# One sine table and its exchanged copy, in a two-dimensional Fourier mix with an RWKV channel mix

## The chip, the cores and the metric

The kernel runs on one core of one Trainium2 chip. The core has five engines that run their own instruction queues in order and meet through semaphores: TensorE (PE: matrix products from SBUF into PSUM, weight loads shown apart as PEld), VectorE (DVE), ScalarE (ACT, with tables for functions such as the sine and the sigmoid), GpSimd (POOL) and SyncE (SP, which only issues transfers here). DMA engines move data between HBM and SBUF; in this kernel the inputs are fetched from GpSimd's queue, except for two small vectors, and the outputs are written from SyncE's. The metric is the device time of one execution in microseconds; lower is better.

## The reference

```python
def _attn_ref(x):                      # x: 8 x 3072 x 256
    X = np.fft.fft(x, axis=1)
    X = np.fft.fft(X, axis=2)
    return X.real.astype(np.float32)

def _moe_ref(x, mu_k, mu_r, w_k, w_v, w_r):
    x_prev = np.concatenate([np.zeros((B, 1, D)), x[:, :-1, :]], axis=1)
    xk = mu_k * x + (1.0 - mu_k) * x_prev
    xr = mu_r * x + (1.0 - mu_r) * x_prev
    k = np.maximum(xk @ w_k, 0.0)      # 256 -> 1024
    v = k * k @ w_v                    # 1024 -> 256
    r = 1.0 / (1.0 + np.exp(-(xr @ w_r)))
    return (r * v).astype(np.float32)
```

The second function takes the output of the first.

## The kernel before

The sequence of 3072 is split into 48 x 64. For each of the 8 batches the Fourier transform is made of products with small tables of sines: `a_sum` (batch 0 and half of batch 1) or `butterfly` and `a_item` (the others) transform over 48 with the table `w_pm`; `d_half` and `d_item` transform over the 256 columns with `w_eo`; `c_item` transforms over the remaining 64 with the tables `m1` and `m2`, which have 27 slots of 64 columns on 128 partitions. Every one of these ends in an eviction from PSUM into SBUF (`evac`, lines 358 to 362) on ScalarE ("A") or VectorE ("V"). `d_item` n fills four of the 24 units of `g_all`, whose columns 0, 257 and 258 to 385 must be zero; `g_zeros` writes these zeros.

`halves` and `diff` then form the transform's rows and their differences, and `scaled` and `mixed` form the mixed inputs x of the channel mix, all on VectorE. The channel mix works on 48 chunks of 512 tokens (three per half `m` of a batch). A chunk takes four steps: each step has a `k_piece` (product with w_k, line 494; relu on ScalarE, line 498), each second step a `square` on VectorE (line 504); the first step of the next chunk has its `r_item` (product with w_r, line 511, sigmoid on ScalarE); and five steps behind, `v_tile` makes the product with w_v (line 523) and `v_out` multiplies by the sigmoid on VectorE and stores.

The order of all instructions is written out by hand. Lines 541 to 578 are the first work of batch 0, up to step 0. From there a table (`at(step, f, ...)`, lines 605 to 671) says which other items go into which step: in a step, `k_piece` comes first, then items on TensorE ("x"), then `v_tile`, then items on VectorE ("w"), then `v_out` and `square`. `pin_order` keeps every engine to this order.

PSUM has three large slots, taken in turn by `ps_w()`, and two small ones, taken in turn by `ps_v()`. A product waits until the eviction of the slot's former content is done. `keep_busy` puts products of zeros into the queue of TensorE between the first items.

The setup comes ahead of line 541. GpSimd issues the loads of batch 0 (line 106), fills `kcol_i` with integers (line 161) and computes angles as integers: for two tables and in two stretches of slots, 0 to 9 (`NS1`) and 9 to 27 (`m_angles`, line 274). VectorE wraps them to one turn (`m_wrap`, line 279) and ScalarE takes the sine (`m_sine`, line 283) into m1 and m2. The two tables differ by the phase that is added: on the lower 64 partitions a quarter and a half turn, on the upper 64 none and a quarter (before half a turn that all have). `m_rest` sets the slots that are exceptions. VectorE also computes `row_i` (lines 235 to 249), the row numbers by which GpSimd gathers w_k, w_r and part of mu (`gather`, line 321): the first half of the weights' rows (`m` = 0) first, then `load_xh(1, 0)`, w_r, w_v, `load_xh(1, 1)` and the other half (lines 324 to 341). `load_xh(b, h)` loads half h of batch b's x in two transfers. The other part of mu goes by six transfers from SyncE.

Of the kernel before, what the change touches and what calls it, by code (L numbers as in the profile page):

```python
# [9 lines left out]
FP32 = mybir.dt.float32  # L10
# [25 lines left out]
def kernel(  # L36
# [101 lines left out]
    def keep_busy(n):  # L138

        ps = ps_w()  # L140
        for _ in range(n):
            nc.tensor.matmul(out=ps[:, 0:512], lhsT=zeros[:, 0:P], rhs=zeros, start=True, stop=True)  # L142
# [37 lines left out]
    for c in range(2):  # L180
        phase(0.25 + 0.25 * c, 0.25 * c)
# [30 lines left out]
    for g in range(2):  # L212
        for n in range(2):
# [15 lines left out]
    V.tensor_scalar(out=rr_f, in0=rr_f, scalar1=float(TURN) / S, scalar2=None, op0=ALU.mult)  # L229

    row_f = const.tile([P, 4], FP32)
    row_i = const.tile([P, 4], UINT32)
    first = const.tile([P, 1], FP32)
    late = const.tile([P, 1], FP32)
    V.tensor_scalar(out=first, in0=pcol_f, scalar1=0.0, scalar2=None, op0=ALU.is_equal)
    V.tensor_scalar(out=late, in0=pcol_f, scalar1=65.0, scalar2=-127.0, op0=ALU.is_ge,
                    op1=ALU.mult)
    V.scalar_tensor_tensor(out=late, in0=pcol_f, scalar=2.0, in1=late, op0=ALU.mult,
                           op1=ALU.add)
    V.tensor_scalar(out=late, in0=late, scalar1=-1.0, scalar2=first, op0=ALU.add, op1=ALU.add)  # L240
    V.tensor_copy(out=row_f[:, 0:1], in_=late)
    V.tensor_scalar(out=late, in0=late, scalar1=-1.0, scalar2=256.0, op0=ALU.mult, op1=ALU.add)
    V.scalar_tensor_tensor(out=row_f[:, 1:2], in0=first, scalar=-128.0, in1=late,
                           op0=ALU.mult, op1=ALU.add)
    V.scalar_tensor_tensor(out=row_f[:, 2:3], in0=first, scalar=-256.0, in1=late,
                           op0=ALU.mult, op1=ALU.add)
    V.scalar_tensor_tensor(out=row_f[:, 3:4], in0=first, scalar=128.0, in1=row_f[:, 0:1],
                           op0=ALU.mult, op1=ALU.add)
    V.tensor_copy(out=row_i, in_=row_f)

    V.memset(mu_f, 0.0)
# [11 lines left out]
    ang = []  # L263
    for nm in ("rl", "k2"):
        t = k2_pool.tile([P, 8, 512], FP16, name=nm, tag=nm)
        ang.append(t.rearrange("p a b -> p (a b)").bitcast(INT32)[:, 0:NSL * 64]
                   .rearrange("p (s t) -> p s t", t=64))
    m1 = const.tile([P, NSL, 64], FP16)
    m2 = const.tile([P, NSL, 64], FP16)
    m_s = const.tile([P, 64], FP16)  # L270
# [450 lines left out]
```

## Time and profile before

| | us |
|---|---|
| median of 14 runs | 470.9 |
| lowest and highest run | 469.98 and 472.45 |
| the profiled execution's own time | 470.13 |
| its span | 468.3 |
| TensorE busy | 453.9 |
| VectorE busy | 358.7 |
| ScalarE busy | 358.3 |
| GpSimd busy | 38.4 |
| start of the first `k_piece` (line 494) | 22.96 |

The profile is of one execution. Times are counted from the start of its span. In the lists in order of time, a line has the start, the length, the engine, the line of the kernel, the operation, what it writes and reads, its count (neighbours are merged), and in brackets how long the engine was idle before it and what ended that. "issue" is idle time that no wait explains. A wait for several things is put down to the one that came last. In the lists by stretch, each engine has its busy time and, in brackets, its number of instructions; the last columns are TensorE's granted clock, the DMA engines' busy share and GB/s. DMA issue on GpSimd counts as its instruction; the transfer itself runs later.

### The profile page before, as it was taken

The numbers are of one execution on the slowest core, as the hardware profiler recorded it, in microseconds if no ns is written. First come the engines' busy times: TensorE is split into PE (matmuls) and PEld (weight loads), VectorE is DVE, ScalarE is ACT, GpSimd is POOL, SyncE is SP. The second block draws the span as 40 slices with busy tenths as digits, with TensorE's granted clock in tenths as the row PEclk, the third lists the DMA queues.
The fourth block names the chain that finished last, engine by engine and source line by source line (L and its number), as shares of the span: only waits on it lengthen the run. The fifth ranks groups of instructions, "written<-read, shape, count | busy, mean of one in ns | idle before, by whom it ended". The sixth has DMA issues, their size and how long they took to land.

```text
span 468.3 us, 10069 instructions
## 1 busy us (share of the span) xinstructions
PE 453.9 (97%) x4258; PEld 333.7 (71%) x4258; DVE 358.7 (77%) x496; ACT 358.3 (77%) x390; POOL 38.4 (8%) x60
## 2 busy tenths in 40 slices
PE   8759999999999999999999999999999999999996
PEld 5537777777777777777777777777777777776774
DVE  7878987987689867887679777897678854898443
ACT  4758898888777887788878887878877888666661
POOL 8850000000000010000000000000000000000000
PEclk9899999999999999999999999999999999999999
DMA  7692752535622365233732356233232222323333
GB/s 134 111 176 43 166 114 68 97 88 116 133 51 64 69 120 129 48 68 67 155 91 51 67 113 137 48 68 69 46 69 46 67 57 57 69 53 82 71 69 90
DMA packets 32561, 40.24 MB, mean 86 GB/s; under 512 B 4164, under 2 KB 30276, under 8 KB 31172
## 3 DMA queue, kind: packets, MB, share of 16 engines
q1 hardware_dynamic: 27812, 25.05, 22.9%
q0 software_dynamic: 4560, 14.42, 18.1%
q8 instruction: 33, 0.54, 0.5%
q10 hardware_dynamic: 144, 0.13, 0.1%
q14 instruction: 12, 0.10, 0.1%
HBM read 28.84 MB, written 25.17 MB: 115 GB/s over the span
## 4 chain that ended last, share of the span: by engine, by line
PE 95%; ACT 3%; DVE 1%; issue 0%; ACTq 0%
PE psV L523 36%; PE psW L494 35%; PE psW L511 9%; PE psW L398 4%; PE psW L425 4%; PE psW L374 4%; PE psW L388 1%; ACT a L362 1%; PE psW L142 1%; ACT pq L362 0%; ACT m L283 0%; ACT L597 0%; DVE y L437 0%; DVE a L360 0%; PE psV L398 0%
## 5 line engine op out<-in xcount | busy, mean ns | idle before, releaser
L498 ACT ACTIVATE rl<-psW 128x1024 f16<-128x1024 f32 x192 | 196.5, 1023 | 87.9 <-PE psW L494 87.9
L494 PE MATMUL psW<-x,wk 128*128 128x512 f16 x768 | 197.2, 379 | 1.8 <-ACT a L362 1.0
L523 PE MATMUL psV<-wv_sb,k 128*128 128x256 f16 x1536 | 198.6, 273 | 0.0
L504 DVE TENSOR_TENSOR k<-rl 128x2048 f16<-128x2048 f16 x96 | 117.4, 1223 | 65.2 <-ACT rl L498 64.6
L523 PEld LDWEIGHTS <-k 128*128 128x128 f16 x1536 | 143.9, 98 | 20.0
L494 PEld LDWEIGHTS <-wk 128*128 128x128 f16 x768 | 74.9, 98 | 52.3 <-issue 2.8
L531 DVE SCALAR_TENSOR_TENSOR o<-psV,r 128x512 f32<-128x512 f32 x96 | 66.1, 689 | 29.1 <-PE psV L523 28.0
L470 DVE TENSOR_TENSOR x<-y,t 128x1536 f16<-128x1536 f16 (+1 forms) x72 | 62.6, 870 | 2.5
L362 ACT ACTIVATE a<-psW 128x768 f16<-128x768 f32 x61 | 49.0, 807 | 6.4 <-PE psW L388 3.9
L511 PE MATMUL psW<-wr,x 128*128 128x256 f16 x384 | 49.8, 273 | 0.0
L516 ACT ACTIVATE r<-psW 128x1024 f16<-128x1024 f32 x48 | 48.9, 1019 | 0.8 <-PE psW L511 0.8
L511 PEld LDWEIGHTS <-x 128*128 128x128 f16 x384 | 37.5, 98 | 14.4 <-DVE x L470 0.2
L362 ACT ACTIVATE g_all<-psW 128x1024 f16<-128x1024 f32 (+1 forms) x46 | 46.7, 1019 | 0.3 <-PE psW L398 0.3
L106 POOL DMA_DIRECT2D xh<-in_x_dram x36 | 18.6, 522 | 242.8 <-DVE eo L119 229.5
L398 PEld LDWEIGHTS <-a 128*128 128x128 f16 x384 | 26.0, 100 | 11.8 <-issue 1.0
L119 DVE TENSOR_TENSOR eo<-xh 96x2048 f16<-96x2048 f16 x26 | 31.5, 1213 | 0.6 <-DMA xh<-in_x_dram 0.6
L374 PEld LDWEIGHTS <-eo 96*128 96x128 f16 x416 | 23.4, 97 | 11.6
L425 PEld LDWEIGHTS <-g_all 128*128 128x128 f16 x648 | 23.9, 99 | 9.3 <-issue 1.7
L362 ACT ACTIVATE pq<-psW 128x896 f16<-128x896 f32 (+5 forms) x33 | 28.6, 867 | 2.3 <-PE psW L398 1.7
L398 PE MATMUL psW<-w_eo,a 128*128 128x128 f16 x376 | 29.0, 222 | 0.7 <-issue 0.7
L425 PE MATMUL psW<-m,g_all 128*128 128x64 f16 x648 | 25.2, 195 | 2.2 <-ACT rl L498 1.4
L374 PE MATMUL psW<-w_pm,eo 96*128 96x96 f16 x416 | 26.3, 205 | 0.0
(87 smaller groups left out, 157.4 us busy)
## 6 DMA issues: line engine op xcount, KB each, us to landing
out_dram<-o SPq DMA_DIRECT2D x191, 128.0 KB, 2.4
xh<-in_x_dram POOLq DMA_DIRECT2D x28, 384.0 KB, 6.1
xh<-in_x_dram POOLq DMA_DIRECT2D x8, 192.0 KB, 5.9
wv_sb<-in_moe_w_v_dram POOLq DMA_DIRECT2D x1, 512.0 KB
out_dram<-o ACTq DMA_DIRECT2D x1, 128.0 KB, 2.8
wk<-in_moe_w_k_dram,row_i POOLq DMA_INDIRECT x4, 10.9
wr<-in_moe_w_r_dram,row_i POOLq DMA_INDIRECT x4, 9.1
mu_f<-in_moe_mu_k_dram SPq DMA_DIRECT2D x1, 0.0 KB
```

Source lines behind the costliest of these rows:

```text
L362: nc.scalar.activation(out=out_ap, in_=in_ap, func=AF.Copy)
L374: nc.tensor.matmul(out=ps[:, 128 * i:128 * i + 96], lhsT=eo[:, 8 * j + i, e, :], rhs=w_pm[0:96, 0], start=True, stop=True)
L398: nc.tensor.matmul(out=_v(ps, 256 * i + 64 * (1 - e), [(128, 2), (1, 64)]), lhsT=a_t[b][:, e, 2 * u:2 * u + 2, :], rhs=w_eo[:, e, :], star ...
L425: nc.tensor.matmul(out=ps[:, o + 64 * i:o + 64 * i + 64], lhsT=g_all[:, u, col:col + 128], rhs=m[:, sl], start=first, stop=last)
L470: V.tensor_tensor(out=dst, in0=_v(y_t[b], 64 * (NSL * a + lo + 3 * m), [(1, n)]), in1=_v(x_t["t", a], 64 * lo, [(1, n)]), op=ALU.subtract ...
L494: nc.tensor.matmul(out=ps[:, 512 * hs:512 * hs + 512], lhsT=wk_sb[m][a][:, 128 * fc:128 * fc + 128], rhs=xk[:, a, 512 * i:512 * i + 512], ...
L498: nc.scalar.activation(out=st["rl"][:, 2 * ds:2 * ds + 2], in_=ps.rearrange("p (f t) -> p f t", f=2), func=AF.Relu, bias=0.0, scale=0.25)
L504: V.tensor_tensor(out=k2_t[c][:, 2 * ds - 2:2 * ds + 2], in0=r, in1=r, op=ALU.mult)
L511: nc.tensor.matmul(out=ps[:, 256 * tb:256 * tb + 256], lhsT=x_t[b, 1, m][:, a, 512 * i + 128 * tb: 512 * i + 128 * tb + 128], rhs=wr_sb[m] ...
L516: nc.scalar.activation(out=st["r", c], in_=ps, func=AF.Sigmoid)
L523: nc.tensor.matmul(out=st["v"][:, 256 * h:256 * h + 256], lhsT=k2_t[c][:, fc, 128 * tb:128 * tb + 128], rhs=wv_sb[:, fc], start=(fc == 0), ...
L531: V.scalar_tensor_tensor(out=o.rearrange("p a b -> p (a b)"), in0=st["v"], scalar=16.0, in1=st["r", c][:, 256 * (tb - 1):256 * (tb + 1)], ...
```

## The change

The second table is no longer computed: `m_swap` makes it from the first, m2's lower 64 partitions being the negative of m1's upper, m2's upper 64 a copy of m1's lower. The angles, wraps and sines are made for one table. `row_i` is written column by column in `rows()`, which comes after the first wrap and sine of the first work; the loads come behind it in `loads()`. The angles of w_eo are made with one operation less, and ahead of the first wrap. The zeros of units 8 to 24 of `g_all` are written by GpSimd, between `load_xh(1, 0)` and the gather of w_r, not by VectorE. The sigmoid's table is loaded before step 0, not in step 1. `keep_busy` takes a small PSUM slot, and one call (of two products) goes. In the steps, `d_item` 4 is evicted by ScalarE, `a_sum(1, 0, 0)` is evicted by VectorE and comes in step 2, and `m_rest(1)` comes in step 0.

```diff
@@ -137,7 +137,7 @@
 
     def keep_busy(n):
 
-        ps = ps_w()
+        ps = ps_v()
         for _ in range(n):
             nc.tensor.matmul(out=ps[:, 0:512], lhsT=zeros[:, 0:P], rhs=zeros, start=True, stop=True)
 
@@ -177,8 +177,7 @@
             phs[lo, hi] = t
         return phs[lo, hi]
 
-    for c in range(2):
-        phase(0.25 + 0.25 * c, 0.25 * c)
+    phase(0.25, 0.0)
 
     pcol_f = const.tile([P, 1], FP32)
     hi48 = const.tile([P, 1], FP32)
@@ -227,28 +226,29 @@
                     op0=ALU.bitwise_and, op1=ALU.logical_shift_left)
     V.tensor_tensor(out=rr_f, in0=pos_h, in1=pos_l, op=ALU.add)
     V.tensor_scalar(out=rr_f, in0=rr_f, scalar1=float(TURN) / S, scalar2=None, op0=ALU.mult)
-
...
-    V.tensor_copy(out=row_i, in_=row_f)
-
-    V.memset(mu_f, 0.0)
+
+    def rows():
+        first = const.tile([P, 1], FP32)
+        late = const.tile([P, 1], FP32)
+        low = const.tile([P, 1], FP32)
+        high = const.tile([P, 1], FP32)
+        V.tensor_scalar(out=late, in0=pcol_f, scalar1=65.0, scalar2=-127.0, op0=ALU.is_ge,
+                        op1=ALU.mult)
+        V.tensor_scalar(out=first, in0=pcol_f, scalar1=0.0, scalar2=None, op0=ALU.is_equal)
+        V.scalar_tensor_tensor(out=late, in0=pcol_f, scalar=2.0, in1=late, op0=ALU.mult,
+                               op1=ALU.add)
+        V.tensor_scalar(out=low, in0=late, scalar1=-1.0, scalar2=first, op0=ALU.add,
+                        op1=ALU.add)
+        V.tensor_scalar(out=high, in0=low, scalar1=-1.0, scalar2=256.0, op0=ALU.mult,
+                        op1=ALU.add)
+        V.tensor_copy(out=row_i[:, 0:1], in_=low)
+        for n, v, by in ((1, high, -128.0), (2, high, -256.0), (3, low, 128.0)):
+            V.scalar_tensor_tensor(out=row_i[:, n:n + 1], in0=first, scalar=by, in1=v,
+                                   op0=ALU.mult, op1=ALU.add)
 
 
     NU = 24
@@ -260,85 +260,90 @@
         V.memset(g_all[:, u0:u1, 0:1], 0.0)
 
 
-    ang = []
-    for nm in ("rl", "k2"):
-        t = k2_pool.tile([P, 8, 512], FP16, name=nm, tag=nm)
-        ang.append(t.rearrange("p a b -> p (a b)").bitcast(INT32)[:, 0:NSL * 64]
-                   .rearrange("p (s t) -> p s t", t=64))
+    ang = (k2_pool.tile([P, 8, 512], FP16, name="rl", tag="rl")
+           .rearrange("p a b -> p (a b)").bitcast(INT32)[:, 0:NSL * 64]
+           .rearrange("p (s t) -> p s t", t=64))
     m1 = const.tile([P, NSL, 64], FP16)
     m2 = const.tile([P, NSL, 64], FP16)
-    m_s = const.tile([P, 64], FP16)
 
     def m_angles(s0, s1):
-        for c in range(2):
-            nc.gpsimd.tensor_scalar(out=ang[c][:, s0:s1], in0=kcol_i[:, s0:s1], scalar1=rr_f,
-                                    scalar2=phase(0.25 + 0.25 * c, 0.25 * c),
-                                    op0=ALU.mult, op1=ALU.add)
-
-    def m_wrap(c, s0, s1):
-        V.tensor_scalar(out=ang[c][:, s0:s1], in0=ang[c][:, s0:s1], scalar1=TURN - 1,
+        nc.gpsimd.tensor_scalar(out=ang[:, s0:s1], in0=kcol_i[:, s0:s1], scalar1=rr_f,
+                                scalar2=phase(0.25, 0.0), op0=ALU.mult, op1=ALU.add)
+
+    def m_wrap(s0, s1):
+        V.tensor_scalar(out=ang[:, s0:s1], in0=ang[:, s0:s1], scalar1=TURN - 1,
                         scalar2=None, op0=ALU.bitwise_and)
 
-    def m_sine(c, s0, s1):
-        nc.scalar.activation(out=(m2 if c else m1)[:, s0:s1], in_=ang[c][:, s0:s1],
-                             func=AF.Sin, bias=m_pi, scale=TWO_PI / TURN)
+    def m_sine(s0, s1):
+        nc.scalar.activation(out=m1[:, s0:s1], in_=ang[:, s0:s1], func=AF.Sin, bias=m_pi,
+                             scale=TWO_PI / TURN)
+
+    lo64, hi64 = slice(0, 64), slice(64, 128)
+
+    def m_swap(s0, s1):
+
+        V.tensor_scalar(out=m2[lo64, s0:s1], in0=m1[hi64, s0:s1], scalar1=-1.0, scalar2=None,
+                        op0=ALU.mult)
+        V.tensor_copy(out=m2[hi64, s0:s1], in_=m1[lo64, s0:s1])
 
     def m_rest(part):
 
 
 
-        h = slice(64, 128)
-        if part == 1:
-            V.tensor_copy(out=m_s[h], in_=m1[h, 25])
-            V.tensor_copy(out=m1[h, 25], in_=m2[h, 25])
-            V.tensor_scalar(out=m2[h, 25], in0=m_s[h], scalar1=-1.0, scalar2=None, op0=ALU.mult)
+        s = 26 if part else 0
+        if part:
+            V.tensor_scalar(out=m2[hi64, 25], in0=m1[hi64, 25], scalar1=-1.0, scalar2=None,
+                            op0=ALU.mult)
+            V.tensor_copy(out=m1[hi64, 25], in_=m1[lo64, 25])
         for m in (m1, m2):
-            s = 26 if part else 0
-            V.tensor_scalar(out=m[h, s], in0=m[h, s], scalar1=-1.0, scalar2=None, op0=ALU.mult)
+            V.tensor_scalar(out=m[hi64, s], in0=m[hi64, s], scalar1=-1.0, scalar2=None,
+                            op0=ALU.mult)
             if part:
-                V.memset(m[0:64, 25], 0.0)
+                V.memset(m[lo64, 25], 0.0)
             else:
-                V.memset(m[h, 1], 0.0)
+                V.memset(m[hi64, 1], 0.0)
                 V.memset(m[:, 0, 0:1], 0.0)
 
+
+    ueo = const.tile([P, 2, 2, 64], INT32)
+    w_eo = const.tile([P, 2, 128], FP16)
+    for c in range(2):
+        V.tensor_scalar(out=ueo[:, :, c], in0=veo_i[:, :, c], scalar1=pd_f,
+                        scalar2=(0.5 + 0.25 * c) * TURN, op0=ALU.mult, op1=ALU.add)
+    V.tensor_scalar(out=ueo, in0=ueo, scalar1=TURN - 1, scalar2=None, op0=ALU.bitwise_and)
     m_angles(0, NS1)
     kcol(NS1, NSL)
-    m_wrap(0, 0, NS1)
-    m_wrap(1, 0, NS1)
-
-    ueo = const.tile([P, 2, 2, 64], INT32)
-    w_eo = const.tile([P, 2, 128], FP16)
-    V.tensor_scalar(out=ueo, in0=veo_i, scalar1=pcol_f, scalar2=float(TURN) / D,
-                    op0=ALU.mult, op1=ALU.mult)
-    for c in range(2):
-        V.tensor_scalar(out=ueo[:, :, c], in0=ueo[:, :, c], scalar1=(0.5 + 0.25 * c) * TURN,
-                        scalar2=None, op0=ALU.add)
-    V.tensor_scalar(out=ueo, in0=ueo, scalar1=TURN - 1, scalar2=None, op0=ALU.bitwise_and)
-    g_zeros(0, 8)
+    m_angles(NS1, NSL)
 
 
     def gather(dst, w, n):
         nc.gpsimd.indirect_dma_start(dst, None, w,
                                      bass.IndirectOffsetOnAxis(ap=row_i[:, n:n + 1], axis=0))
 
-    m_angles(NS1, NSL)
-    for a in range(2):
-        gather(wk_sb[0][a], moe_w_k, a)
-    mus = [mu.rearrange("(a b) -> a b", b=1) for mu in (moe_mu_k, moe_mu_r)]
-    for i, mu in enumerate(mus):
-        nc.sync.dma_start(out=mu_f[0:1, 0, i:i + 1], in_=mu[0:1])
-        nc.sync.dma_start(out=mu_f[1:65, 0, i:i + 1], in_=mu[1:129:2][0:64])
-        nc.sync.dma_start(out=mu_f[65:128, 0, i:i + 1], in_=mu[2:128:2])
-        gather(mu_f[:, 1, i:i + 1], mu, 1)
-    load_xh(1, 0)
-    for a in range(2):
-        gather(wr_sb[0][a], moe_w_r, a)
-    nc.gpsimd.dma_start(out=wv_sb, in_=moe_w_v.rearrange("(fc p) v -> p fc v", p=128))
-    load_xh(1, 1)
-    for a in range(2):
-        gather(wk_sb[1][a], moe_w_k, 2 + a)
-    for a in range(2):
-        gather(wr_sb[1][a], moe_w_r, 2 + a)
+    def loads():
+
+        V.memset(mu_f, 0.0)
+        mus = [mu.rearrange("(a b) -> a b", b=1) for mu in (moe_mu_k, moe_mu_r)]
+        for i, mu in enumerate(mus):
+            nc.sync.dma_start(out=mu_f[0:1, 0, i:i + 1], in_=mu[0:1])
+            nc.sync.dma_start(out=mu_f[1:65, 0, i:i + 1], in_=mu[1:129:2][0:64])
+            nc.sync.dma_start(out=mu_f[65:128, 0, i:i + 1], in_=mu[2:128:2])
+        for a in range(2):
+            gather(wk_sb[0][a], moe_w_k, a)
+        for i, mu in enumerate(mus):
+            gather(mu_f[:, 1, i:i + 1], mu, 1)
+        load_xh(1, 0)
+        nc.gpsimd.memset(g_all[:, 8:24, 258:GU], 0.0)
+        for c in (0, 257):
+            nc.gpsimd.memset(g_all[:, 8:24, c:c + 1], 0.0)
+        for a in range(2):
+            gather(wr_sb[0][a], moe_w_r, a)
+        nc.gpsimd.dma_start(out=wv_sb, in_=moe_w_v.rearrange("(fc p) v -> p fc v", p=128))
+        load_xh(1, 1)
+        for a in range(2):
+            gather(wk_sb[1][a], moe_w_k, 2 + a)
+        for a in range(2):
+            gather(wr_sb[1][a], moe_w_r, 2 + a)
 
     def eo_sine():
         nc.scalar.activation(out=w_eo.rearrange("p a b -> p (a b)"),
@@ -541,32 +546,34 @@
 
     a_sum(0, 0, 0)
     a_sum(0, 0, 4)
+    m_wrap(0, NS1)
+    m_sine(0, NS1)
+    rows()
+    loads()
     keep_busy(3)
     a_sum(0, 0, 8)
     a_sum(0, 0, 12)
-    m_sine(0, 0, NS1)
-    m_sine(1, 0, NS1)
+    eo_sine()
+    m_swap(0, NS1)
+    g_zeros(0, 8)
+    m_wrap(NS1, NSL)
     keep_busy(2)
     a_sum(0, 1, 0)
-    m_wrap(0, NS1, NSL)
+    m_sine(NS1, NSL)
+    eo_rest()
     a_sum(0, 1, 4, "V")
-    eo_sine()
-    m_sine(0, NS1, NSL)
     keep_busy(2)
     a_sum(0, 1, 8, "V")
-    eo_rest()
     m_rest(0)
     a_sum(0, 1, 12)
-    keep_busy(2)
     d_half(0, 0, ps_v(), "A")
     d_half(0, 2, ps_v(), "V")
     d_half(0, 4, ps_w(), "A")
     d_half(0, 6, ps_w(), "V")
-    m_wrap(1, NS1, NSL)
+    m_swap(NS1, NSL)
     c_item(0, 0, 5)
     halves(0, 0, 5)
     c_item(0, 5, 4)
-    m_sine(1, NS1, NSL)
     halves(0, 5, 9)
     diff(0, 0, 8)
     d_item(0, 2)
@@ -574,7 +581,7 @@
         scaled(0, 0, 0, a, 0, 8)
         mixed(0, 0, 0, a, 0, 8)
     d_item(0, 3)
-    g_zeros(8, 24)
+    nc.scalar.activation(out=pd_f, in_=m_pi, func=AF.Sigmoid)
     keep_busy(6)
 
 
@@ -590,11 +597,6 @@
         for a in range(2):
             V.tensor_copy(out=mu_m[:, a], in_=mu_f[:, 1 - a])
         V.tensor_copy(out=mu_m[0:1], in_=mu_f[0:1])
-
-    warm = const.tile([P, 1], FP32)
-
-    def sigmoid_table():
-        nc.scalar.activation(out=warm, in_=m_pi, func=AF.Sigmoid)
 
     chunks = [(b, m, i) for b in range(B) for m in range(2) for i in range(3)]
     nk = 4 * len(chunks)
@@ -605,14 +607,13 @@
 
     at(0, c_item, 0, 9, 8)
     at(0, mix2, 0, 1, 0, 0, 8)
+    at(0, m_rest, 1)
     at(0, halves, 0, 9, 17)
     at(0, diff, 0, 8, 16)
-    at(1, sigmoid_table)
-    at(1, d_item, 0, 4, "V")
-    at(1, a_sum, 1, 0, 0)
+    at(1, d_item, 0, 4)
     at(1, mix2, 0, 0, 0, 8, 16)
     at(2, d_item, 0, 5)
-    at(2, m_rest, 1)
+    at(2, a_sum, 1, 0, 0, "V")
     at(3, c_item, 0, 17, 8)
     at(3, butterfly, 1, 1, 0)
     at(4, halves, 0, 17, 25)
```

## The prediction

> **What bounds the kernel now.** I read the first page, then the engines stretch by stretch, then the order of time of each engine up to 60 us, then the DMA packets by the microsecond.
>
> The page: the span is 468.3 us and TensorE is busy in nearly all of it.
>
> ```profile
> span 468.3 us, 10069 instructions
> PE 453.9 (97%) x4258; PEld 333.7 (71%) x4258; DVE 358.7 (77%) x496; ACT 358.3 (77%) x390; POOL 38.4 (8%) x60
> ```
>
> Busy time by stretch (length, then TensorE, weight loads, VectorE, ScalarE, GpSimd, granted clock, DMA share):
>
> ```profile
> 30.00:36.00 6.00, 2.50 (x31) 1.44 (x30) 5.14 (x14) 4.36 (x6) 0.53 (x1) 1.00 0.99 182
> 36.00:42.00 6.00, 6.00 (x58) 4.39 (x55) 4.63 (x9) 5.04 (x6) 0.00 (x0) 1.00 0.03 5
> 48.00:60.00 12.00, 12.00 (x115) 8.99 (x113) 11.83 (x18) 10.07 (x12) 0.00 (x0) 1.00 0.64 143
> ```
>
> From 36 us on TensorE has no idle time until the last microseconds. The change touches only what comes earlier, so its worth is how much earlier TensorE passes the places where something else can still hold it. The 48 to 60 row names that something: VectorE is busy 11.83 of 12.00 us there. In order of time:
>
> ```profile
> 35.19 1.22 DVE L119 TENSOR_TENSOR eo<-xh 96x2048 f16<-96x2048 f16 x1 [0.58 <-DMA xh<-in_x_dram]
> 36.71 1.23 DVE L504 TENSOR_TENSOR k<-rl 128x2048 f16<-128x2048 f16 x1 [0.30 <-ACT rl L498]
> 40.33 0.96 DVE L360 CAST a<-psW 128x768 f16<-128x768 f32 x1 [1.00 <-PE psW L388]
> 54.98 0.43 DVE L470 TENSOR_TENSOR x<-y,t 128x512 f16<-128x512 f16 x1
> 55.38 1.04 PE L511 MATMUL psW<-wr,x 128*128 128x256 f16 x8
> 55.46 0.68 PEld L511 LDWEIGHTS <-x 128*128 128x128 f16 x7 [0.20 <-DVE x L470]
> ```
>
> The reader should see a second chain beside TensorE's. VectorE waits for batch 1's second half of x (`load_xh(1, 1)`), which lands at about 35.15. From 35.19 it works until 55.41, when it delivers the x that `r_item` of step 12 loads as weights. That is 20.22 us, of which only 0.30 and 1.00 are idle. TensorE's weight load waits for this x without any room. So TensorE cannot pass step 12 earlier by more than VectorE does, and VectorE starts that run at the landing.
>
> Why the landing is at 35: DMA packets in the microseconds that start at 23, 28, 31, 34 and 35. The total less the last count is the number of packets of 8 KB and more, which only x has (96 for each half).
>
> ```profile
> DMA packets 55, 0.15 MB, mean 154 GB/s; under 512 B 10, under 2 KB 38, under 8 KB 38
> DMA packets 178, 0.24 MB, mean 239 GB/s; under 512 B 12, under 2 KB 158, under 8 KB 158
> DMA packets 34, 0.17 MB, mean 175 GB/s; under 512 B 8, under 2 KB 9, under 8 KB 14
> DMA packets 222, 0.19 MB, mean 194 GB/s; under 512 B 26, under 2 KB 165, under 8 KB 221
> DMA packets 128, 0.09 MB, mean 86 GB/s; under 512 B 21, under 2 KB 117, under 8 KB 127
> ```
>
> `load_xh(1, 0)` ends in microsecond 23 (17 large packets). wr and wv (small packets) follow, the next x half starts at 28 (20 large) and is nearly over at 31 (20), but single packets follow at 34 and 35[...]. Transfers run in the order in which GpSimd issues them:
>
> ```profile
> 8.77 1.14 POOL L161 IOTA kcol_i<- 128x1152 int32 x1
> 12.97 1.34 POOL L321 DMA_INDIRECT wk<-in_moe_w_k_dram,row_i  x1 [0.16 <-DVE ueo L316]
> 18.11 1.14 POOL L106 DMA_DIRECT2D xh<-in_x_dram  x2
> 19.56 1.48 POOL L321 DMA_INDIRECT wr<-in_moe_w_r_dram,row_i  x1 [0.30 <-DMA wk<-in_moe_w_k_dram,row_i]
> 22.81 0.98 POOL L336 DMA_DIRECT2D wv_sb<-in_moe_w_v_dram  x1
> 23.75 1.08 POOL L106 DMA_DIRECT2D xh<-in_x_dram  x2
> 32.44 1.28 ACT L597 ACT_TABLE_LOAD   x1
> ```
>
> **The change, up to step 4.** Before, `k_piece` of step 4 starts at 36.19, and the first one at 22.96.
>
> *GpSimd.* Two angle operations go (1.09 and 1.33 us, L274), so wk0 can be issued at about 12.97 - 2.4 = 10.6. `rows` now runs after the first wrap (about 9.2, below) and needs some 0.8 us to its first column at 0.15 to 0.2 each: ready at 10.1, not late. mu's six SP loads move with it, from 7.8 to about 10.5; landing took 3.1 to 4.4, so they are there by 17.5, and the first use (22.00 before) is near 20. SP issues nothing else until 47.
>
> *Wrap and sines.* The first wrap is on VectorE behind ueo. L314's two equal operations took 0.24 and 1.05 us: the slow one ended when a GpSimd operation did (11.49). The wrap may so wait for the second iota (7.75 to 8.9) and end at 9.2, else at 8.3. ScalarE then has, from 8.66 or 9.25: sine 0.67, two evictions 1.51, w_eo 0.45, eviction 0.75, sine 1.25, eviction 0.81, about 5.4 us, so the first `d_half` can start at 14.1 to 14.9 instead of 16.83. PSUM no longer holds it, as `keep_busy` is in other banks. I take 14.9, 1.9 earlier. The swaps (64 rows, 576 and 1152 long) cost, by L457 (512 long 0.35, 1536 long 0.60), about 0.36 and 0.5 each, two of each: 1.7 us; they stand where wraps of 0.5 to 1.4 and 0.76 stood. The six fewer VectorE instructions (0.15 to 0.2 each, and the 0.55 cast) lie in time that waits on ScalarE: nothing.
>
> *The zeros of units 8 to 24* go from VectorE (0.91 us, and TensorE waited for them to 24.77) to GpSimd, between xh and wr: 16 x 128 halfwords. No row shows a large GpSimd memset; the nearest is the iota, 0.65 us for 576 and 1.14 for 1152: 0.85 ns an element, so 2048 cost 1.9 us, with the two small ones 2.2. [...] I take 2.2, since the iota has no inputs either. [...]
>
> [...] The memset runs from about 16.9 to 18.9, the second swap is due at 17.5, [...] What would be late next is step 4, and that is covered (below): 0 either way. Without the cover it costs 1.6.
>
> *Steps 0 to 4.* First `k_piece` at 22.96 - 1.9 = 21.1. The sigmoid table (1.28 + 0.20, between two evictions at 32.44 before) comes after `d_item` 3, at 20.9 to 22.4, ahead of the first relu at 22.6, since the 1.25 us sine that stood there is gone. From 22.6 ScalarE has eight evictions of 1.03 (four relu, two `d_item`, two `c_item`; `d_item` 4 is now its own, `a_sum` is VectorE's): to 30.85. Step 4 starts at about 29.9, 6.3 earlier. VectorE does its mixes, then the `a_sum` eviction at 29.0 to 29.9, and then stands before the butterfly of `load_xh(1, 1)`. `m_rest(1)` (1.2 us), now ahead, is in that time too.
>
> **What of the 6.3 is left.** VectorE is ready for the butterfly at 30 [...], the data is not. wk and `load_xh(1, 0)` come 2.4 earlier, so that half ends at 21.5, but wr, wv and the next half are issued only 2.4 - 2.2 = 0.2 earlier (wr 19.4, wv 22.6, xh 23.5). Ahead of wv the queue was full before [...]; now wv moves as soon as issued, about 0.9 us after 22.6 as xh did, and behind wr's second part: 23.7 to 23.9. So the landing advances by 0.8 to 1.5; I take 1.1: 34.05. From there VectorE's queue is the same as before, without the 0.30 and 1.00 of idle, since ScalarE and TensorE are ahead: 20.22 - 1.30 = 18.92, x at 52.97 instead of 55.41. TensorE unheld would be there at 55.38 - 6.3 = 49.1. Gain: 1.1 + 1.3 = 2.4 us; the other 3.9 become idle time of TensorE in steps 5 to 12. Later VectorE products had room (second squares of a chunk done at 49.18, needed at 50.27), so nothing is lost or won behind it. The 2 dropped `keep_busy` matmuls lie in waits: 0.
>
> Sum on the profiled execution: 470.13 (468.3 span, 1.83 around it) - 2.4 = 467.7. Its median is 0.77 above it, so I forecast 470.9 - 2.4 = 468.5.
>
> **Rivals.**
> 1. *The landing lets go.* The straggler is this execution's accident: without it the half lands near 32 before, and VectorE was anyway busy to 34.61. With the large packets over at about 31 in the new one: 34.61 - 31.2 + 1.3 = 4.7, at most the 6.3: 464.6 to 466.5. For it: most of that half's packets were over by 32. Against: the last one was not.
> 2. *A transfer that was not moved.* GpSimd's memsets at 3.7 to 5.5 us: the landing advances by 1.1 + 2.2 less that, -0.4 to -2.2, and the gain is within 0.9: 470 to 471.8. [...] The halved table would then do what it says and be worth nothing.
> 3. *Slower.* GpSimd's memset, at its place ahead of wr, delays the landing. From a price of 2.2 + 1.1 + 1.3 = 4.6 us it decides the sign, from 5.5 measurably; at 6.5 the time is 472.8. [...]
>
> **How the numbers follow.** Main case 0.56 (own range 467.2 to 469.6), rival 1 0.27, rival 2 0.12, rival 3 0.05. A change under 0.2% (0.94 us) is about what a measurement of this kernel cannot tell from none. Main and rival 1 are faster, 0.83; rival 2 same, 0.12; rival 3 slower, 0.05. The range leaves out the far end of rival 1 and the half of rival 2 with rival 3: 465.3 to 470.3.
>
> **What would show it.** Right: first `d_half` near 14.9; table load ahead of the first relu; step 4 near 30; VectorE idle for 3 to 5 us before the first butterfly, ended by DMA; then no idle for 18.9 us; TensorE idle in steps 5 to 12. GpSimd memset near 1.9 us. Wrong: if the butterfly waits for nothing, or starts before 33, rival 1 holds; if the memsets take over 3.7 us, 2 or 3; if step 4 starts after 33, the upstream sum is wrong.

## The result, and the profile after

The changed kernel takes 468.17 us (467.58 to 469.22), the kernel before, on the same chip, 471.05 (469.32 to 472.54). The ratio is 0.9938, with a 95% interval of 0.9924 to 0.9951: faster by 0.6%, some 2.9 us, where 2.4 were forecast. The profiled execution took 468.9 with a span of 467.1: its gain on the execution shown before (span 468.3) is only 1.2. A second profile of the same kernel (`e9_after_again`, below) has a span of 465.1 and so a gain of 3.2. Why the two differ is most of what follows.

The page of the changed kernel:

```profile
span 467.1 us, 10062 instructions
PE 452.8 (97%) x4256; PEld 332.1 (71%) x4256; DVE 358.1 (77%) x491; ACT 357.2 (76%) x388; POOL 37.2 (8%) x61
```

The busy sums hardly move. The stretches do (length, then TensorE, weight loads, VectorE, ScalarE, GpSimd, granted clock, DMA share, GB/s):

```profile
24.00:30.00 6.00, 5.75 (x51) 3.70 (x51) 4.51 (x15) 4.03 (x4) 4.41 (x5) 0.72 1.17 179
30.00:36.00 6.00, 5.24 (x55) 3.52 (x55) 3.38 (x6) 5.38 (x7) 0.00 (x0) 1.00 0.84 149
36.00:42.00 6.00, 5.62 (x54) 4.21 (x52) 5.90 (x11) 4.03 (x6) 1.10 (x2) 1.00 0.21 23
48.00:60.00 12.00, 11.34 (x101) 8.00 (x100) 11.83 (x17) 9.38 (x11) 0.00 (x0) 1.00 0.53 121
```

Two things are new. From 36 us on, TensorE was never idle before; now it is, by 0.38 and 0.66 us in the last two rows, while VectorE is busy 5.90 of 6 and 11.83 of 12. And in the first row TensorE's granted clock is 0.72, where it was 1.00 in the same stretch before; looked at more finely, it is 0.50 from 24.7 to 28.1 us. The order of time on VectorE and TensorE shows the first of the two:

```profile
35.56 1.22 DVE L119 TENSOR_TENSOR eo<-xh 96x2048 f16<-96x2048 f16 x1 [2.58 <-DMA xh<-in_x_dram]
36.70 1.22 DVE L509 TENSOR_TENSOR k<-rl 128x2048 f16<-128x2048 f16 x1
37.98 0.61 PE L528 MATMUL psV<-wv_sb,k 128*128 128x256 f16 x4 [0.26 <-DVE k L509]
39.23 0.95 DVE L365 CAST a<-psW 128x768 f16<-128x768 f32 x1
53.56 0.28 PE L516 MATMUL psW<-wr,x 128*128 128x256 f16 x1 [0.21 <-DVE x L475]
53.80 0.43 DVE L475 TENSOR_TENSOR x<-y,t 128x512 f16<-128x512 f16 x1
54.29 0.94 PE L516 MATMUL psW<-wr,x 128*128 128x256 f16 x7 [0.44 <-DVE x L475]
```

VectorE stood 2.58 us before the butterfly of `load_xh(1, 1)`, until the DMA ended. It then ran without a gap from 35.56 to 54.23, 18.67 us (18.92 were predicted), and TensorE waited for it in step 5 (the `v_tile` at 37.98) and at `r_item` of step 12. The chain of waits of this execution says the same: it goes from GpSimd's issue through the transfer into VectorE.

```profile
23.38 0.51 POOL xh L106
23.89 11.57 DMA xh<-in_x_dram
35.56 1.22 DVE eo L119
```

So in this execution the landing held the kernel, as forecast. But it came at 35.5, not at 34.05. GpSimd's queue, in order of time:

```profile
11.29 1.07 POOL L320 DMA_INDIRECT wk<-in_moe_w_k_dram,row_i  x1 [0.78 <-DVE mu_f L325]
16.67 1.14 POOL L106 DMA_DIRECT2D xh<-in_x_dram  x2
17.75 1.88 POOL L336 MEMSET g_all<- 128x2048 f16 x1
19.88 1.14 POOL L320 DMA_INDIRECT wr<-in_moe_w_r_dram,row_i  x1
22.40 0.99 POOL L341 DMA_DIRECT2D wv_sb<-in_moe_w_v_dram  x1
23.34 1.09 POOL L106 DMA_DIRECT2D xh<-in_x_dram  x2
```

The half is issued 0.41 us earlier than before (23.75) and lands 0.4 later. Its large packets by the microsecond (the microseconds 27, 30 and 34; total less the last count):

```profile
DMA packets 199, 0.23 MB, mean 234 GB/s; under 512 B 13, under 2 KB 181, under 8 KB 181
DMA packets 42, 0.17 MB, mean 174 GB/s; under 512 B 2, under 2 KB 22, under 8 KB 22
DMA packets 173, 0.11 MB, mean 110 GB/s; under 512 B 25, under 2 KB 164, under 8 KB 171
```

18, 20 and, at 34, still 2: the bulk starts one microsecond earlier than before (27 instead of 28) and is over by 31, but a few packets straggle as they did before, and the landing is that of the last one.

The second new thing is upstream. These are VectorE and TensorE from the first wrap to step 4:

```profile
7.95 1.38 DVE L274 TENSOR_SCALAR rl<-rl 128x576 int32<-128x576 int32 x1 [0.65 <-POOL rl L270]
9.43 1.08 DVE L242 SCALAR_TENSOR_TENSOR late<-pcol_f,late 128x1 f32<-128x1 f32 x1
15.41 0.61 PE L403 MATMUL psV<-w_eo,a 128*128 128x128 f16 x8 [1.71 <-ACT m L278]
17.90 2.21 DVE L285 TENSOR_SCALAR m<-m 64x1152 f16<-64x1152 f16 x1
20.13 0.45 DVE L287 COPY m<-m 64x1152 f16<-64x1152 f16 x1
23.28 0.38 PE L499 MATMUL psW<-x,wk 128*128 128x512 f16 x1 [2.70 <-DVE x L475]
25.92 1.90 PE L499 MATMUL psW<-x,wk 128*128 128x512 f16 x4
33.20 1.03 PE L499 MATMUL psW<-x,wk 128*128 128x512 f16 x4
```

The last line is step 4: 33.20, against 36.19 before and 29.9 predicted. Three operations are longer than their kind: an operation on one column of 1.08 us (L242), the swap of 2.21 (its twin, the copy of the same shape, takes 0.45), and after TensorE's idle 2.70 us a `k_piece` of 1.90 instead of 1.03.

### The profile page after: what moved, and what is told of

It is laid out like the page before. It is cut to its first block, busy times and chain, and to the rows that moved or that the text cites. A ratio compares the mean times of both kernels' runs of the same rounds, so it can differ in the third digit from the quotient of the medians.

```text
span 467.1 us, 10062 instructions
## 1 busy us (share of the span) xinstructions
PE 452.8 (97%) x4256; PEld 332.1 (71%) x4256; DVE 358.1 (77%) x491; ACT 357.2 (76%) x388; POOL 37.2 (8%) x61
## 4 chain that ended last, share of the span: by engine, by line
PE 87%; DVE 5%; POOL 3%; DMA 2%; issue 1%; POOLq 0%; DVEq 0%
PE psV L528 35%; PE psW L499 33%; PE psW L516 9%; PE psW L403 4%; PE psW L430 4%; PE psW L379 4%; DMA xh<-in_x_dram 2%; POOL xh L106 1%; DVE k L509 1%; DVE x L475 1%; DVE t L462 1%; DVE eo L119 1%; POOL wr L320 0%; POOL mu_f L320 0%; DVE o L536 0%
## 5 line engine op out<-in xcount | busy, mean ns | idle before, releaser
L367 ACT ACTIVATE g_all<-psW 128x1024 f16<-128x1024 f32 (+1 forms) x47 | 47.7, 1019 | 0.3 <-PE psW L403 0.2
```

Of the source, the lines that this page charges most:

```text
L367: nc.scalar.activation(out=out_ap, in_=in_ap, func=AF.Copy)
```

## The experiments

The line numbers in the lists are those of each kernel, and shift by a few. Theory L says that the landing of `load_xh(1, 1)` and VectorE's run behind it hold the kernel. Theory U says that the work upstream, up to step 4, does. The runs were made on several chips, and the kernel before had medians of 470.58 (e1 to e4), 469.56 (e5 to e8), 470.03 (e9 to e11) and 468.86 (e12); so kernels that ran on different chips are compared by their ratio to before.

**e1 and e2: the half issued early.** Both kernels, with `load_xh(1, 1)` directly behind `load_xh(1, 0)`:

```diff
         load_xh(1, 0)
+        load_xh(1, 1)
         nc.gpsimd.memset(g_all[:, 8:24, 258:GU], 0.0)
...
-        load_xh(1, 1)
```

> The changed kernel, with load_xh(1, 1) issued directly behind load_xh(1, 0), ahead of the zeros, w_r and w_v. Landing theory (the wait of VectorE's first butterfly for that half of x sets the time): the half is issued 4.5 us earlier, the butterfly waits no more for a DMA, TensorE's waits for VectorE at step 5 and at r_item of step 12 are gone, and the span is shorter by about what TensorE lost there: step 4 at 33.2 against 36.19 leaves 3.0 us over the kernel before's span, 465.3, a time near 467.1. Upstream theory (the gain is what the first work saves, and the landing of the profiled execution was its accident): the profile shows the earlier landing, the median stays at 468.2 within 0.3.

> The kernel before, with the same edit: load_xh(1, 1) directly behind load_xh(1, 0). Landing theory: in the profile of before TensorE was full from 36.19 on and VectorE lost only 0.58 us to the landing, so a like execution gains nothing; the median gains what executions with a later landing lose, 0 to 0.9 us: 470.2 to 471.05. If the landing alone made the difference between the two kernels, this one would reach 468.2. Upstream theory: 471.05, unchanged.

Measured: e1 467.94 us, ratio 0.9948 (0.9928 to 0.9969); e2 470.62, ratio 1.0006 (0.9992 to 1.0019). In e1 no wait for DMA is left, and TensorE isn't held later, but the time hardly falls. The order of time of e1:

```profile
18.92 2.37 DVE L287 COPY m<-m 64x1152 f16<-64x1152 f16 x1
23.98 0.38 PE L499 MATMUL psW<-x,wk 128*128 128x512 f16 x1 [3.61 <-DVE x L475]
33.90 1.21 DVE L119 TENSOR_TENSOR eo<-xh 96x2048 f16<-96x2048 f16 x1
34.04 1.02 PE L499 MATMUL psW<-x,wk 128*128 128x512 f16 x4 [0.56 <-DVE a L365]
```

Step 4 starts at 34.04, and 36.19 - 34.04 = 2.15 is the difference of the spans (468.3 and 466.1). With the landing out of the way, U alone sets the time, and it gives no more than the changed kernel (2.4 us by the ratio). So the 6.3 us that I had given TensorE upstream fall. The edit itself made U a little worse: GpSimd's memset now runs from 18.64 to 20.79, and the two operations of the swap take 1.21 and 2.37 us, against 2.21 and 0.45. The second, from 18.92, ends 0.50 behind the memset; the first starts at 17.69, ahead of it, and what stretched it is not shown. Step 4 is 0.84 later than in the changed kernel. For the kernel before, the time did not change, as U had it and L allowed: without U moved, an early landing is worth nothing.

**e3: the zeros not on GpSimd.** The zeros of units 8 to 24 go to VectorE near 1.7 us, behind its first constants, where it waits for loads; GpSimd's three memsets go.

```diff
+    g_zeros(8, 24)
...
         load_xh(1, 0)
-        nc.gpsimd.memset(g_all[:, 8:24, 258:GU], 0.0)
-        for c in (0, 257):
-            nc.gpsimd.memset(g_all[:, 8:24, c:c + 1], 0.0)
```

> The changed kernel, with the zeros of units 8 to 24 written by VectorE near 1.7 us, where it waits for GpSimd, and none by GpSimd. Landing theory: w_r, w_v and the half of x are issued 2.2 us earlier, the half lands 1.5 to 2.2 earlier, r_item of step 12 too: a time of 466.0 to 466.8, VectorE still waiting for the DMA. The lock on the second swap (2.21 us instead of 0.45) goes too, and the first k_piece is near 21.3 instead of 23.28; by the landing theory that gain is hidden. Upstream theory: the same 2 us come from the first k_piece, and VectorE's butterfly would then wait for nothing.

Measured: 466.21, ratio 0.9915 (0.9893 to 0.9937). Both theories had it there. Its order of time shows what moved:

```profile
17.84 0.45 DVE L288 TENSOR_SCALAR m<-m 64x1152 f16<-64x1152 f16 x1
21.45 0.38 PE L499 MATMUL psW<-x,wk 128*128 128x512 f16 x1 [0.93 <-DVE x L475]
26.73 1.02 PE L499 MATMUL psW<-x,wk 128*128 128x512 f16 x4 [1.73 <-issue]
32.39 1.22 DVE L119 TENSOR_TENSOR eo<-xh 96x2048 f16<-96x2048 f16 x1 [0.62 <-DMA xh<-in_x_dram]
```

With no memset on GpSimd the swap takes 0.45, not 2.21: the memset held it up, for 1.76 us. In the changed kernel the swap starts at 17.90, beside the memset (17.75 to 19.63), and ends at 20.11, 0.48 behind the memset's end; in e9 (below) it takes 2.80 and ends 0.49 behind it. TensorE is idle 0.93 instead of 2.70 ahead of the first `k_piece`, and its clock stays at 1.00 in 24 to 30. Transfers behind the zeros are issued 1.8 us earlier. Step 4 is at 31.82; it would be earlier still without 1.73 us in which TensorE waits for nothing that the profile shows (VectorE has 1.83 of the same at the same time). What stalled them is not known.

**e4: the sigmoid's table in step 1 again**, by the same instruction.

```diff
     d_item(0, 3)
-    nc.scalar.activation(out=pd_f, in_=m_pi, func=AF.Sigmoid)
     keep_busy(6)
...
+    at(1, sigmoid_table)
```

> The changed kernel, with the sigmoid table loaded in step 1 again, as before the change. Landing theory: 1.48 us more for ScalarE between two evictions, step 4 at about 34.5, and the half of x lands when it did: the time stays within 0.3 us of the changed kernel's 468.2. Upstream theory: 1.3 to 1.5 us slower, 469.6.

Measured: 469.16 (467.89 to 469.87), ratio 0.9965 (0.9952 to 0.9977): by the ratios 1.3 us more than the changed kernel (0.9938), or 0.7 if its second measurement is taken (0.9950, e9 below). L's forecast, within 0.3 us of the changed kernel, failed against the first measurement, and U's figure was near; against the second the intervals overlap. The table load (1.28 us) stands between two evictions at 30.30, and step 4 is at 34.38 instead of 33.20, 1.2 us later. Thus the table's new place, which I had put under the cover, is probably a part of the gain.

**e9: the changed kernel once more, unedited.**

> The changed kernel once more, for a second profile. By what e1, e3 and e4 showed, two chains join at r_item of step 12: VectorE's from the landing of load_xh(1, 1), and TensorE's from the first k_piece (its memset lock and its lowered clock). Expected: a ratio to before of 0.993 to 0.995, and in the profile either a wait for the half of x of over 2 us with step 12 held by VectorE, or a wait under 1 us with step 4 near 33.2 to 34 and TensorE never held afterwards. If neither is seen, the account of two chains is wrong.

Measured: 466.89 (466.13 to 468.87), ratio 0.9950 (0.9930 to 0.9970). In its profile, by the order of time, the other theory holds (the first line is all of step 0's `k_piece`):

```profile
23.26 2.17 PE L499 MATMUL psW<-x,wk 128*128 128x512 f16 x4 [3.29 <-DVE x L475]
32.98 1.03 PE L499 MATMUL psW<-x,wk 128*128 128x512 f16 x4
33.54 1.22 DVE L119 TENSOR_TENSOR eo<-xh 96x2048 f16<-96x2048 f16 x1 [0.68 <-DMA xh<-in_x_dram]
```

The half lands two microseconds earlier than in the first profile, VectorE waits only 0.68 for it, and TensorE isn't held by it in any later step. Step 4 is at 32.98, and 36.19 - 32.98 = 3.21 is the difference of the spans (3.2). The granted clock in 24 to 30 is 0.59; it is 0.50 from 22.0 to 28.9. So one and the same kernel is held by L in one execution and by U in another.

**e5 and e10: e1 with more products of zeros ahead of the first `k_piece`**, 11 in e5 and 19 in e10, to see what the lowered clock costs.

```diff
-    keep_busy(6)
+    keep_busy(11)
```

> The kernel of e1 (half of x early) with 11 in place of 6 products of zeros ahead of the first k_piece, to fill TensorE's idle 3.6 us there. Clock theory (TensorE's idle time ahead of the first k_piece is what lowers its granted clock to 0.72 from 24 to 30 us): the clock of that stretch is near 1.0, the c_item and the second k_piece are 1.0 to 1.7 us shorter, step 4 is 0.9 to 1.4 us earlier than its 34.04, and the time is 466.5 to 467.0. If the clock doesn't set the start of step 4, because ScalarE's eight evictions do: 467.9, as e1.

> The kernel of e1 with 19 products of zeros ahead of the first k_piece: in e5 the 11 took only 2.5 us at full clock and left 2.0 us idle, and the clock still fell. 19 leave less than 0.9 us. Clock theory: granted clock 1.0 from 24 to 30 us, the second k_piece 1.03 instead of 1.90 us, step 4 at 32.7 to 33.2 instead of 34.04, time 0.9 to 1.4 us below e1's (a ratio of 0.992 to 0.993). Otherwise as e1, 0.995.

Measured: e5 467.46, ratio 0.9956 (0.9940 to 0.9971). The 11 products took only 2.54 us, TensorE was still idle for 1.99, and the clock was again 0.72: the premise wasn't met. e10: 466.44 (466.41 to 466.45), ratio 0.9933 (0.9909 to 0.9957). The stretch of e10 from 24 to 30, columns as above, has the full clock:

```profile
24.00:30.00 6.00, 5.41 (x60) 3.47 (x61) 5.42 (x18) 4.56 (x6) 4.78 (x5) 1.00 1.22 184
```

And its order of time:

```profile
18.74 4.26 PE L142 MATMUL psV<-zeros 128*128 128x512 f16 x19
23.97 0.38 PE L499 MATMUL psW<-x,wk 128*128 128x512 f16 x1 [0.96 <-DVE x L475]
32.53 1.02 PE L499 MATMUL psW<-x,wk 128*128 128x512 f16 x4 [0.57 <-DVE a L365]
```

The first `k_piece` starts where it did in e1 (23.98), step 4 comes 1.5 us earlier (34.04 in e1), and the span is 1.5 shorter. By the ratios to before it is 0.7, with intervals that overlap. So the filled idle time is worth 0.7 to 1.5 us. That all of it is the clock is not shown, and the profile of e5 speaks against it. These are ScalarE's first eviction of a `c_item` behind the first relu, in e1 and then in e5, and step 4 of e5:

```profile
27.87 1.02 ACT L367 ACTIVATE pq<-psW 128x1024 f16<-128x1024 f32 x1 [1.39 <-PE psW L430]
26.39 1.02 ACT L367 ACTIVATE pq<-psW 128x1024 f16<-128x1024 f32 x1
32.68 1.03 PE L499 MATMUL psW<-x,wk 128*128 128x512 f16 x4
```

The clock is 0.50 for 3.4 us in both, from 25.6 in e1 and from 25.7 in e5, and the second `k_piece` takes 1.90 us in both. But in e5 ScalarE doesn't wait, and step 4 is at 32.68, only 0.15 us behind e10's with its full clock. (This was the fastest of e5's six executions; the others took 0.75 to 0.93 longer.) A wait of this kind also stands in the profile of before, at full clock: by the trace the `c_item` ends at 25.66, and its eviction starts at 27.17. So e1 holds both a lowered clock and a wait of ScalarE, and e10 neither; no run parts them, and what causes the wait stays open.

**e6: the kernel before with five products of zeros in steps 2 and 3**, made as `keep_busy` makes them but in a small PSUM slot.

```diff
+    at(2, keep_warm, 2)
+    at(3, keep_warm, 3)
```

> The kernel before, with 2 products of zeros at the end of step 2 and 3 ahead of the c_item of step 3, in a small PSUM slot, where TensorE idles. Clock theory: the spread of the kernel before (468.9 to 472.5) is a lowered TensorE clock that falls, in some executions, into the stretch after 36 us where TensorE is full; with the idle time filled the spread shrinks below 1.5 us and the median comes to 469.0 to 469.8. Landing theory for the spread: unchanged, 470.6 with the same spread.

Measured: 468.15, ratio 0.9971 (0.9962 to 0.9981). The runs lie within 467.88 to 468.87, where those of before on the same chip went from 467.92 to 470.57. So most of before's spread went with the products, and 1.4 us of its median, half of what the whole change gains. What they change is argued and not shown. The profile of e6 has the full clock up to the last microseconds. That of before has 0.50 from 17.0 to 20.4, but this lies ahead of the products (29.33 to 32.1), which cannot have removed it; that of e2, without the products, has 0.50 from 34.8 to 38.2, behind the place where they stand, which fits the clock theory. Step 4 is at 34.17, and now the landing takes over, as the order of time shows:

```profile
35.21 1.22 DVE L119 TENSOR_TENSOR eo<-xh 96x2048 f16<-96x2048 f16 x1 [2.56 <-DMA xh<-in_x_dram]
53.94 0.94 PE L517 MATMUL psW<-wr,x 128*128 128x256 f16 x7 [0.30 <-DVE x L476]
```

**e7: e1 and e3 together** (the half early, the zeros on VectorE).

> e1 and e3 together: zeros by VectorE near 1.7 us, and load_xh(1, 1) directly behind load_xh(1, 0). Landing theory: in e3 the butterfly still waited 0.62 us for the DMA in its profile, and more in its slower executions; without that wait every execution is at e3's lower end, 465.7 within 0.3, and the spread of e3 (465.7 to 467.2) is gone. Upstream theory: the median of e3, 466.2.

Measured: 463.37 (463.35 to 463.47), ratio 0.9869 (0.9852 to 0.9886), less than either kernel of the case and less than both theories had. Its order of time:

```profile
20.76 0.38 PE L499 MATMUL psW<-x,wk 128*128 128x512 f16 x1 [0.93 <-DVE x L475]
29.34 1.21 DVE L119 TENSOR_TENSOR eo<-xh 96x2048 f16<-96x2048 f16 x1
29.47 1.02 PE L499 MATMUL psW<-x,wk 128*128 128x512 f16 x4 [0.71 <-DVE a L365]
```

With the swap's operations at 0.44 and 0.45 us, the clock at 1.00 from 12 to 60 us and no wait for the transfer, step 4 starts at 29.47. My sum for it was 29.9. Against e3 (31.82) the first `k_piece` is 0.69 earlier, and the stall of 1.73 is not there; that it would go nobody had foreseen, and why it went is not known.

**e8 and e11: the second table computed again**, in the changed kernel's order (e8) and in e7's (e11). The angles are made for both tables as before; the swaps make way for wraps and sines.

```diff
-    m_swap(0, NS1)
+    m_wrap(1, 0, NS1)
+    m_sine(1, 0, NS1)
...
-    m_swap(NS1, NSL)
+    m_wrap(1, NS1, NSL)
...
+    m_sine(1, NS1, NSL)
```

> The changed kernel with the second table computed again (two more GpSimd operations on angles of 1.1 and 1.3 us, two wraps in place of the four swaps, two more sines of 0.7 and 1.25 us on ScalarE, one of them ahead of the sigmoid table), all else as changed: rows late, zeros on GpSimd, sigmoid table early. Landing theory: the gathers and the half of x are issued about 1.6 us later (2.4 less the 0.8 that GpSimd idled before the first gather), the half lands that much later, 469.5 to 470. Rival, that the new order made the gain and not the table: 468.2 to 468.6.

> The kernel of e7 (zeros early on VectorE, half of x early) with the second table computed again as in e8. With no wait for the landing and no memset on GpSimd, what is left of the second table is ScalarE's two sines, 0.7 and 1.25 us, the longer one ahead of the sigmoid table and the first relu, and GpSimd's 2.4 us, of which 0.8 were idle. Expected: 1 to 2 us above e7, a ratio to before of 0.989 to 0.991. If the order alone makes e7's gain: 0.987 as e7. If the table is worth more than its sines: above 0.992.

Measured: e8 468.01, ratio 0.9973 (0.9963 to 0.9983); e11 463.74, ratio 0.9871 (0.9844 to 0.9897). By the ratios, the halved table is worth 0.23 to 0.35% (1.1 to 1.6 us) in the changed kernel's order, and little in e7's (0.9871 and 0.9869; the spans, 462.0 and 461.6, say 0.4 us). The landing theory held for e8: 0.9973 of the 471.05 us of before is 469.8. The expectation for e11, 1 to 2 us, was wrong. The order of time of e8 tells why it is worth something there:

```profile
32.08 1.02 PE L498 MATMUL psW<-x,wk 128*128 128x512 f16 x4 [0.59 <-DVE a L364]
35.13 1.22 DVE L119 TENSOR_TENSOR eo<-xh 96x2048 f16<-96x2048 f16 x1 [3.11 <-DMA xh<-in_x_dram]
```

Step 4 is not later than in the changed kernel (32.08, against 33.20 and 32.98), but the half is issued at 25.11 instead of 23.34, and VectorE waits 3.11 for it. GpSimd's two more angle operations sit ahead of all transfers; with the half issued early they hardly matter.

**e12: e7 with `rows()` ahead of the first wrap.**

```diff
+    rows()
     m_wrap(0, NS1)
     m_sine(0, NS1)
-    rows()
     loads()
```

> The order of e7 (zeros early, load_xh(1, 1) directly behind load_xh(1, 0)), and now rows() stands ahead of the first m_wrap instead of behind it. Theory that the last of rows()' operations, kept off by GpSimd's angle operation, is on the path: in e7 that operation takes 1.08 us and GpSimd idles 0.78 us before the first gather. Ahead of the wrap, rows() lies in time in which VectorE waits for the iota anyway: gathers about 0.8 us earlier, second wrap and the 1152 long sine 0.7 earlier, the first d_half at about 14.6 instead of 15.30, step 4 about 0.7 before e7's 29.47, and 0.5 to 0.8 us less than e7: ratio 0.985 to 0.986. Rival: the first d_half is set by ScalarE's chain of the first sine and the evictions, which the wrap ahead of it starts later; then nothing or a loss of up to 0.8: ratio 0.987 to 0.989.

Measured: 462.95 (462.75 to 463.20), ratio 0.9871 (0.9855 to 0.9888). The profile is as the theory had it: the operation takes 0.44 us instead of 1.08, the first gather is issued at 10.56 instead of 11.18, the first `d_half` starts at 14.66 instead of 15.30, step 4 at 28.88 instead of 29.47, and the span is 461.0 instead of 461.6. The ratio doesn't show it, and taken alone it lies where the rival had it: 0.6 us is 0.13%, less than its interval.

No run takes back the other parts of the change alone: the moves in the steps, the PSUM slot of `keep_busy`, the angles of w_eo. What each is worth is not known.

**One sum for all profiles.** Let A be the start of step 4 and L the start of that butterfly. With 432.1 us behind A (read from before: 468.3 - 36.19) and 431.5 behind L (from after: 467.1 - 35.56), the later of the two gives the span of every kernel but one (those of before and after by construction, the others as a test):

| kernel | A | L (VectorE's wait) | A + 432.1 | L + 431.5 | span |
|---|---|---|---|---|---|
| before | 36.19 | 35.19 (0.58) | **468.3** | 466.7 | 468.3 |
| after | 33.20 | 35.56 (2.58) | 465.3 | **467.1** | 467.1 |
| e9 | 32.98 | 33.54 (0.68) | **465.1** | 465.0 | 465.1 |
| e1 | 34.04 | 33.90 (none) | **466.1** | 465.4 | 466.1 |
| e3 | 31.82 | 32.39 (0.62) | **463.9** | **463.9** | 464.0 |
| e4 | 34.38 | 34.22 (0.69) | **466.5** | 465.7 | 466.5 |
| e6 | 34.17 | 35.21 (2.56) | 466.3 | **466.7** | 466.8 |
| e7 | 29.47 | 29.34 (none) | **461.6** | 460.8 | 461.6 |
| e8 | 32.08 | 35.13 (3.11) | 464.2 | **466.6** | 466.6 |
| e10 | 32.53 | 32.40 (none) | **464.6** | 463.9 | 464.6 |

Where VectorE has no wait, L is set by VectorE's own queue and not by a landing. e5, e11 and e12 fit too. The exception is e2 (A 35.31, span 468.9, 1.5 more than the sum): there the clock is 0.50 from 34.8 to 38.2, from step 4 on, where the `k_piece` takes 1.90 and `r_item` 1.61 (0.87 and 0.57 more than elsewhere).

## Why the prediction was right, and where it was not

**VectorE's run behind the landing, and its join with TensorE at step 12: right**, in the execution that was profiled first. 18.67 us against 18.92, no gap, TensorE idle in steps 5 and 12. But it idled for 1.0 us and not for the 3.9 of the sum, since step 4 itself was late. The table above shows that this second chain holds in three of the profiles (after, e6, e8) and comes within 0.1 us of holding in two more (e3, e9).

**The landing: right in kind, wrong in size.** "The landing advances by 0.8 to 1.5; I take 1.1" stood for 0.2 us of earlier issue and 0.9 of a queue that wv no longer meets; the 0.9 was my estimate, as no view shows wv's packets apart from wr's. The issue came 0.41 earlier, the landing at 35.5 (0.4 later) in one profile and 33.5 (1.7 earlier) in the other. The bulk of the packets did come about one microsecond earlier; the last ones, which end the transfer, did not. A single landing of a transfer that straggles by itself was taken for a fixed point. I had seen the straggler and made it rival 1; it is neither this rival nor the main case, but a spread of two microseconds between two profiles of the changed kernel. (That rival's gain of 4.7 makes 466.2, not the 466.5 of its range.)

**Step 4 at 29.9: wrong, and the largest error.** It was 33.20 and 32.98. "If step 4 starts after 33, the upstream sum is wrong" was my own sign for it. The working itself was near (e7: 29.47, with the zeros on VectorE and the half issued early); what it priced at nothing was not nothing:
- "0 either way" for a second swap that GpSimd's memset holds up. The 1.6 us that it would cost "without the cover" was an estimate: the memset's expected end, 18.9, less the 17.5 at which the swap was due, and 0.2 by which its two operations were to be longer than the wrap in their place. All that the profile of before had for it was L314's pair (0.24 and 1.05 us, the slow one ending with GpSimd's operation at 11.49). The swap lost 1.76. The step that failed is the cover: I subtracted this loss from a slack of 3.9 us that existed only if nothing else was late too.
- "ready at 10.1, not late" for `rows`. Its third operation took 1.08 us instead of 0.16 and ended with GpSimd's angle operation at 10.51, and GpSimd itself waited 0.78 for the rows (wk at 11.29 instead of 10.6). The second wrap and the longer sine stand behind, and the first `d_half` was at 15.41 and not at 14.9; with the rows moved ahead it came 0.64 earlier (e12 against e7).
- These two make the first `k_piece` 2.2 us late (23.28 against 21.1), and so TensorE idle for 2.70 (3.29 in the second profile). Its clock was lowered there (0.50 from 24.7 to 28.1; from 22.0 to 28.9 in the second): steps 0 to 4 took 9.9 instead of 8.8 (9.7 in the second). The wait of ScalarE seen in e1 is here too in the first profile (0.7 us), not in the second. I had not considered the clock at all, although the profile of before shows 0.80 in 18 to 24, and its first `k_piece` at 22.96, from which I counted, is 0.8 later than in e2 and e6, which have 1.00 there.

**GpSimd's memset: right.** 1.88 us where the iota's row gave 1.9. Rivals 2 and 3 needed memsets of 3.7 us and more, a price that no trace shows, and fell with it.

**The sigmoid's table ahead of the first relu: right** (20.89 to 22.17), but its leaving step 1 was worth 0.7 to 1.3 us (e4), which I had put among the 3.9 lost. **The two dropped products at 0:** no run tells. e6 and e10 only show that such products can be worth something near idle time.

**The sum, 468.5 against 468.17**, is near in part by luck. The landing, which alone was to set the time, gave 1.2 us in the execution where it held; in the other it came early enough for 3.3, and there the upstream held, with 3.2 of the 6.3 that I had given it. The forecast of 2.4 lies between the two. The medians also hold what no profile here explains: the runs of before spread over 3.2 us, those of the changed kernel over 1.6. How many executions each arm holds, the runs don't tell: there are two profiles, one of each.

## What to carry to other kernels

Before an edit is priced at nothing because a later wait covers it, add up everything that was covered by the same slack; here a swap held up, a late row and a slower run through the steps each fell into it, and together they used up 3.3 of 3.9 us. Where two chains join, write both as a start plus a constant tail and take the later one: it was exact to 0.1 us in all profiles but one, and it says at once that moving the arm that is not the later gains nothing (e2), that moving the later one gains until the other takes over (e6), and that both together gain more (e7, 6.2 us against before on the same chip). Watch idle time of TensorE ahead of dense products, and the granted clock behind it (3.61 us and 0.72 in e1): shortening it to 0.96 us with products of zeros left the first `k_piece` where it was (23.97, and 23.98 in e1), with a clock of 1.00, and gave 0.7 to 1.5 us (e10 against e1).

## What the runs showed of the hardware that was not expected

- TensorE's clock after short idle times. Idle times of 0.93 and 0.96 us ahead of the first `k_piece` left the clock at 1.00 (e3, e7, e10); with 1.99 (e5), 2.70 (after), 3.29 (e9) and 3.61 us (e1) it was 0.72, 0.72, 0.59 and 0.72 from 24 to 30, with single `k_piece`s of 1.90 to 2.17 us instead of 1.03. The lowered clock comes in stretches: it is 0.50 for 3.4 us (24.7 to 28.1 in after, 25.6 to 29.0 in e1, 17.0 to 20.4 in before) or for twice that (22.0 to 28.9 in e9, where it fell while TensorE was still idle). Their start differs between two executions of one kernel, 24.7 in after and 22.0 in e9. With the idle time shortened by products of zeros from 3.61 to 0.96 us the clock stayed at 1.00 (e10 against e1). But in before it fell at 17.0 behind idle times of only 1.05 and 0.47 us (ahead of 15.11 and 16.83); what idle time is enough, and what else sets the clock, no run tells.
- An operation on one element per partition was held up. `scalar_tensor_tensor` on 128 x 1 (L242) took 1.08 us beside GpSimd's longer angle operation and 0.44 when it met the shorter one (e12); both times it ended when GpSimd's operation did (10.51 and 7.82). Operations of the same kind and size took 0.16 in before, where two of them fell into the first 0.3 us of an angle operation of GpSimd, so there the first 0.3 us held nothing up. Why it is held up is not shown.
- The first wrap's time differed with what GpSimd did beside it: it took 1.38 us beside GpSimd's iota (after, e7) and 0.46 beside an angle operation of GpSimd (e8, e11), which itself took 1.11 where its like took 0.93.
- Two microseconds of spread in the landing of one transfer of the same kernel (33.5 and 35.5), from issues 0.02 us apart (23.34 and 23.32).
